# Spectral mixing and a SiLU block: the 32-point transforms of batches 2 to 7 on sums and differences of n and 31-n

## The chip, the cores and the metric

The kernel runs on one core of a Trainium2 chip. The metric is the device time of one execution in microseconds (us). A core has five engines with a queue each: TensorE (matrix products; PE in the profile, with its weight loads as PEld), VectorE (DVE), ScalarE (ACT), GpSimd (POOL) and SyncE (SP, which here only starts transfers). TensorE writes its results to eight banks of PSUM, from where VectorE or ScalarE copies them out. All numbers here are 32-bit floats; each product in the program becomes two matmul records in the profile.

## The reference

```python
# x: (8, 3008, 256), filt_r, filt_i: (1505, 256)
X = np.fft.rfft(x, axis=1)
Y = X * (filt_r + 1j * filt_i)[None]
y = np.fft.irfft(Y, n=3008, axis=1)          # (8, 3008, 256)
# w_in: (256, 2048), w_out: (2048, 256)
h = y.reshape(24064, 256) @ w_in
out = (h * (1 / (1 + np.exp(-h)))) @ w_out
```

Along the sequence of each batch a Fourier transform, a product with a complex filter and the inverse transform; then a two-layer block with SiLU on all 24064 rows.

## The kernel before

**The main stream.** The second part is cut into 48 pairs of token blocks (6 per batch: two halves of the batch, three blocks in each, of 256, 256 and 240 columns), and each pair into 8 steps over the 2048 hidden units: 384 steps, 48 per batch. A step has two generators that take turns in eight rounds (0 to 7): `hidden(step)` (L765) makes 7 products with the first weights into the banks x (`px`) and yz (`pyz`), and `project(step - 1)` (L824) makes 7 products of the step before with the second weights into four accumulators a0 to a3 (`acc`). A 2x2 block product is made from 7 instead of 8 products, so sums and differences run on VectorE in each step: three combines of `pyz` with copied `px` (`g<-pyz,abc`: g0, g2, g1 in that order), one of 512 columns and two more (`finish`, L813). ScalarE makes the copies of `px` and SiLU. With the last step of a pair the accumulators are copied out (`drain`, L849) and GpSimd adds them up (7 additions); SP stores the result. `tokens(pair)` (L755) makes the sums that a new pair needs, on VectorE, at fixed places (L1201).

**The transforms of the next batch** are cut into pieces that are put between these rounds: `put(step, round, piece)`. A piece is emitted into the engines' queues at that place, and each engine works through its queue in order. For batch b, places are relative to step 48 b, so that place -36 lies in the stream of batch b - 1. A sequence of 3008 = 94 x 32 is transformed in two stages each way:

- first forward stage, 94 points: for batches 2 to 7 in three "fold" groups f (`fold`, `stage1_fold`, `evict_fold`; tile `pf`) and two plain groups u = 6, 7 (`stage1`, `evict_t1`; tile `pa`). The products are copied to SBUF (tiles `tf`, `t`), and GpSimd's queue stores them to DRAM as d1[parity, s, re/im, n, channel], n = 0 to 31.
- second forward stage, 32 points over n: `load_t2(g)` (SP's queue) fetches 4 values of s with 64 partitions (re/im and n), and `forward(g)` (L476; tile `pb`) makes 16 products of 64x32 tiles into two banks, for each g of 6. `multiply` and `add` (L495, L514; VectorE) apply the filter.
- first inverse stage, 32 points: `inverse(g, 2)` (L520; tile `pc`) makes 32 products of 32x64 tiles for two g into four banks a0, f, a1, f. `even` (L568) copies two of them on ScalarE, `rows` (L573) makes sums and differences with the other two on VectorE, and GpSimd's queue stores them to DRAM as d2[row, n, h, channel].
- second inverse stage: `load_t4(g)` fetches four n for all rows, `stage3(g)` (L596; tile `pd`) makes 32 products and `evict_y` copies them into `y`, the input of the main stream.

**Order around the change.** PSUM has two free banks ("f"); other pieces borrow banks of the main stream. `open_step(step, pieces)` emits its pieces at the start of a step, after the first two products of `project`, and holds `project` in rounds 0 and 2, so that x and yz (`HIDDEN`) are free for them. Pieces at round 7 of a step that is a multiple of 8 run between two pairs, when accumulators are free; if the step is in `joined`, the next pair's `project` takes a0 and a1 first and a2 later (L833), otherwise a2 first (L836).

```python
        rest = 5 if b == 1 else 6
        open_step(at - 36, *last_part[0](rest), (part["forward"], 0))
        for g, step in ((0, -32), (2, -24), (4, -16)):
            put(at + step, 7, part["inverse"], g, 2)
            if g < 4:
                pending.append((at + step + 7 / ROUNDS, 10 ** 6 + 9, lambda g=g: part["forward"](g + 2, ACCS)))
                joined.add(at + step)
            put(at + step, 7, part["even"], g, 0, 2)
            put(at + step, 7, part["even"], g, 1, 2)
            put(at + step + 1, 5, part["rows"], g, 0, 2)
            put(at + step + 2, 3, part["rows"], g, 1, 2)
```

So step -36 holds `stage3(6)` of the batch before and `forward(0)`; `forward(1)`, `(3)`, `(5)` stand alone in rounds of -35, -27, -20; `forward(2)` and `(4)` follow the inverse in the joined steps -32 and -24 (at -32 with `stage3(7)` between); the inverse at -16 stands alone.

## Time and profile before

| | us |
|---|---|
| three runs | 2574.51, 2575.43, 2577.16 (median 2575.43) |
| span of the profiled execution | 2578.9 |
| first step of the main stream starts | about 81 |
| one batch in the steady part (48 steps) | 312.6, 312.3 |
| L841 `acc`, TensorE busy | 1509.0 |
| L778 `px`, `pyz`, TensorE busy (four groups) | 679.2 + 454.0 + 232.7 + 225.7 |
| L608 `pd`, of which from `t` tiles | 67.3 |
| L509 `multiply`, VectorE busy | 61.6 + 61.3, 90 each of 684 and 681 ns |
| L578 `rows`, VectorE busy | 57.4, 84 of 683 ns |
| L570 `even`, ScalarE busy | 22.5, 42 of 589 ns alone |
| granted TensorE clock, mean | 0.995 |

How to read it: "busy" is the time in which at least one instruction of a group runs; matmuls overlap, so the mean of one (some 380 ns for 256 columns) is not its pace. The timeline has the start and the length of each instruction or run of like instructions, in us from the start of the span, then the engine, the line, what is written and read, and in brackets how long the engine stood idle before and what ended it. A shape such as 64*32 is the part of TensorE's 128x128 array that a matmul takes.

### The profile page before, as it was taken

What the parts mean: (1) busy time and instruction counts of PE and PEld (TensorE: products, weight loads), DVE (VectorE), ACT (ScalarE), POOL (GpSimd) and SP (SyncE); (2) the same over time, 40 slices, a digit from 0 to 9 for tenths busy, and PEclk for the clock granted to TensorE, in tenths of its full rate; (3) what the DMA queues carried; (4) which work ended last, traced back from release to release, by engine and by line L of the source; (5) the groups of instructions that cost most, each with busy time, mean ns of one, the idle gap of its engine ahead of it and who ended that gap; (6) DMA issues with size and microseconds to landing.
All of it is one profiled execution on the core that took longest, in us unless ns stands there. A gap on an engine that the chain in (4) does not pass through costs nothing.

```text
span 2578.9 us, 47033 instructions
## 1 busy us (share of the span) xinstructions
PE 2552.5 (99%) x18810; PEld 2194.7 (85%) x18810; DVE 1594.2 (62%) x3397; ACT 1085.9 (42%) x3009; POOL 427.3 (17%) x670
## 2 busy tenths in 40 slices
PE   8899999999999999999999999999999999999998
PEld 6688888888888888888888888888888888888987
DVE  7866656666666666666656665666665666545544
ACT  2544444444444444444444434444444444444443
POOL 3211111121112111211122111211121112101101
PEclk9899999999999999999999999999999999999999
DMA  9521132222222212222123121321132210200000
GB/s 285 160 65 62 55 84 64 60 75 65 58 63 73 90 38 58 76 77 74 50 58 92 48 74 50 84 76 55 57 82 62 74 42 28 68 14 16 16 9 17
DMA packets 117316, 170.98 MB, mean 66 GB/s; under 512 B 15332, under 2 KB 91076, under 8 KB 116212
## 3 DMA queue, kind: packets, MB, share of 16 engines
q1 hardware_dynamic: 96920, 117.05, 16.3%
q0 software_dynamic: 17328, 45.76, 5.6%
q10 hardware_dynamic: 2848, 5.15, 0.7%
q8 instruction: 148, 2.42, 0.4%
q14 instruction: 72, 0.59, 0.1%
HBM read 96.07 MB, written 81.26 MB: 69 GB/s over the span
## 4 chain that ended last, share of the span: by engine, by line
PE 96%; DMA 3%; ACT 0%; DVE 0%; issue 0%; ACTq 0%; SPq 0%; POOL 0%; POOLq 0%; DVEq 0%
PE acc L841 44%; PE px L778 26%; PE pyz L778 19%; PE pd L608 3%; PE pb L487 2%; PE pc L530 2%; PE pf L454 1%; DMA d<-q 0%; PE pa L374 0%; DMA w_t<-in_x_dram 0%; DMA filt<-in_filt_r_dram 0%; DMA w_t<-d 0%; PE pa L365 0%; DMA d_t<-d_tbl 0%; DMA raw<-in_moe_w_out_dram 0%; DMA t<-d 0%
## 5 line engine op out<-in xcount | busy, mean ns | idle before, releaser
L841 PE MATMUL acc<-g,w_t 128*128 128x256 f32 (+1 forms) x5376 | 1509.0, 375 | 0.4 <-DVE g L749 0.4
L841 PEld LDWEIGHTS acc<-g,w_t 128*128 128x128 f32 x5376 | 1021.6, 190 | 115.8 <-DVE g L749 0.8
L749 DVE TENSOR_TENSOR g<-pyz,abc 128x256 f32<-128x256 f32 (+1 forms) x1152 | 480.0, 417 | 689.3 <-ACT abc L799 395.0
L749 DVE TENSOR_TENSOR g<-g 128x256 f32<-128x256 f32 (+3 forms) x1152 | 599.6, 521 | 196.7 <-ACT g L782 183.6
L778 PE MATMUL px<-ty,w_t 128*128 128x256 f32 (+1 forms) x2304 | 679.2, 376 | 1.1 <-ACT abc L793 0.6
L782 ACT ACTIVATE g<-g 128x256 f32<-128x256 f32 (+1 forms) x1152 | 472.9, 410 | 250.1 <-DVE g L749 250.1
L749 POOL TENSOR_TENSOR s<-s 128x256 f32<-128x256 f32 (+1 forms) x331 | 257.3, 794 | 1768.1 <-DVE s L859 1555.2
L778 PEld LDWEIGHTS px<-ty,w_t 128*128 128x128 f32 x2304 | 433.2, 190 | 64.4 <-issue 6.2
L778 PE MATMUL pyz<-y,w_t 128*128 128x256 f32 (+1 forms) x1536 | 454.0, 377 | 0.0
L778 PEld LDWEIGHTS pyz<-y,w_t 128*128 128x128 f32 x1536 | 283.8, 189 | 47.5 <-DVE g L749 7.0
L793 ACT COPY abc<-px 128x256 f32<-128x256 f32 (+1 forms) x384 | 141.3, 368 | 372.8 <-PE px L778 372.8
L799 ACT COPY abc<-px 128x256 f32<-128x256 f32 (+1 forms) x384 | 141.5, 368 | 338.6 <-PE px L778 337.6
L782 ACT ACTIVATE g<-px 128x256 f32<-128x256 f32 (+1 forms) x384 | 145.8, 380 | 300.7 <-PE px L778 300.7
L778 PE MATMUL px<-y,w_t 128*128 128x256 f32 (+1 forms) x768 | 232.7, 385 | 0.8 <-DVE y L622 0.8
L778 PE MATMUL pyz<-ty,w_t 128*128 128x256 f32 (+1 forms) x768 | 225.7, 376 | 0.2 <-DVE g L749 0.2
L778 PEld LDWEIGHTS px<-y,w_t 128*128 128x128 f32 x768 | 140.4, 190 | 33.0 <-DVE y L628 5.8
L778 PEld LDWEIGHTS pyz<-ty,w_t 128*128 128x128 f32 x768 | 144.6, 190 | 18.8 <-DVE g L749 1.0
L786 ACT COPY abc<-px 128x256 f32<-128x256 f32 (+1 forms) x384 | 135.3, 352 | 52.6 <-PE px L778 52.6
L608 PEld LDWEIGHTS pd<-wi_t,t 48*64 48x64 f32 x3840 | 61.4, 135 | 25.3 <-ACT g L782 16.4
L466 POOL DMA_DIRECT2D d<-tf x144 | 71.4, 503 | 29.7 <-DVE tf L462 29.7
L859 ACT COPY s<-acc 128x512 f32<-128x512 f32 (+1 forms) x94 | 54.2, 577 | 47.6 <-issue 28.6
L582 POOL DMA_DIRECT2D d<-q x84 | 45.7, 547 | 149.6 <-DVE q L578 146.8
(135 smaller groups left out, 1212.9 us busy)
## 6 DMA issues: line engine op xcount, KB each, us to landing
t<-d SPq DMA_DIRECT2D x120, 192.0 KB
t<-d SPq DMA_DIRECT2D x84, 256.0 KB
d<-q POOLq DMA_DIRECT2D x84, 256.0 KB, 2.7
out_dram<-s SPq DMA_DIRECT2D x64, 256.0 KB
d<-tf POOLq DMA_DIRECT2D x144, 96.0 KB, 4.0
xr<-in_x_dram SPq DMA_DIRECT2D x6, 1472.0 KB
out_dram<-s SPq DMA_DIRECT2D x30, 240.0 KB
x_all<-in_x_dram SPq DMA_DIRECT2D x72, 96.0 KB
```

Source lines behind the costliest of these rows:

```text
L466: nc.gpsimd.dma_start(out=d1[k // 2, :, k % 2, n0:n0 + 4], in_=us["tf"][32 * k:32 * k + NS].rearrange("p q n c -> p (q n) c"))
L487: nc.tensor.matmul(out=ps[k][32 * j:32 * j + 32, ri, :], lhsT=d_t[rows, 4 * g + at, ri, :], rhs=rhs, start=True, stop=True)
L530: nc.tensor.matmul(out=ps[j][64 * k:64 * k + 64, a, :], lhsT=e_t[rows, g + a, k, ri, :], rhs=zs[k][rows, ri, :], start=(a == 0 and ri == 0 ...
L608: nc.tensor.matmul(out=ps[h][c0:c0 + 64, cb, i, :], lhsT=t4[rows, i, 128 * cb + c0:128 * cb + c0 + 64], rhs=wi_t[rows, :], start=True, sto ...
L749: eng.tensor_tensor(out=out, in0=in0, in1=in1, op=op)
L778: nc.tensor.matmul(out=out, lhsT=w_t[:, jp, c, 0], rhs=rhs, start=start, stop=True, skip_group_check=True)
L782: nc.scalar.activation(out=g[:, k, 0:n], in_=g[:, k, 0:n] if src is None else src, func=AFT.Silu)
L786: nc.scalar.copy(out=sums[:, 0, 0:n], in_=xo)
L793: nc.scalar.copy(out=sums[:, 1, 0:n], in_=xo)
L799: nc.scalar.copy(out=sums[:, 2, 0:n], in_=xo)
L841: nc.tensor.matmul(out=acc[pair][i][:, h, 0:n], lhsT=w_t[:, jp, c, 1], rhs=g[:, k, 0:n], start=(jp == 0 and h == 0), stop=last, skip_group ...
L859: copy(out=s[:, 2 * i:2 * i + 2, 0:n], in_=acc[pair][i][:, :, 0:n])
```

## The change

Batches 0 and 1 stay as they are. For batches 2 to 7 the values at n and 31 - n are added and subtracted before the 32-point stage, so that each half of them needs 16 cosines or sines in place of 32, for the real and the imaginary part on partitions of their own:

- First stage: the fold groups now hold n = 4f to 4f+3 and their mirror images, and the plain groups u = 6, 7 are mirror images of each other. `evict_fold` copies two of the four banks on ScalarE; `pairs_fold` makes differences and sums with the other two on VectorE (`butterfly`, two operations of 512 columns for each of two halves), and GpSimd's queue stores both (8 stores at once, of the same size as the 8 in two lots before). `pairs_t1` does the same for u = 6, 7 (4 operations on VectorE instead of a copy on VectorE and one on ScalarE for u = 7; 6 stores instead of 4 for the two).
- `forward_two(g)`, for g = 0, 2, 4, takes two groups at once: 32 products of 32x32 tiles into four banks (f, f, x, yz), in opened steps at -36, -28, -20. `free_two` copies the banks x and yz to SBUF on ScalarE. `multiply_two` (8 operations of 512 columns) and `add_two` (4 of 512 instead of 8 of 256) are spread over the step and the three after it.
- `inverse_two(g)` makes 32 products of 32x32 tiles for two groups into four banks, at the places of the old `inverse`, with all three steps joined. `even_two` and `rows_two` are `even` and `rows`; `ends_two` makes the sum and the difference that give n and 31 - n (4 more operations of 512 columns per two groups on VectorE), and the stores follow it.
- `stage3(6)` moves from step -36 to the joined step before (-32), with `stage3(7)`; `stage3` of the second half runs in mirrored order with another table. `load_t4(0)` and `(1)` are issued at -12 instead of -14. Three tables are loaded over the old ones at step 40.

```diff
+        def butterfly(p, q, ps):
+            back = ps[:, ::-1, :]
+            nc.vector.tensor_tensor(out=q, in0=p, in1=back, op=ALU.subtract)
+            nc.vector.tensor_tensor(out=p, in0=p, in1=back, op=ALU.add)
...
+        def forward_two(g):
+            ps = {(k, ri): bank(b, f"pb_{b}_{g}_{k}_{ri}", HIDDEN[ri] if k else None)
+                  for k in range(2) for ri in range(2)}
+            for a in range(2):
+                for j in range(4):
+                    for k in range(2):
+                        par, at = slot_source(k, j)
+                        for ri in range(2):
+                            rows = slice(64 * par + 32 * ri, 64 * par + 32 * ri + 32)
+                            nc.tensor.matmul(out=ps[k, ri][32 * j:32 * j + 32, a, :],
+                                             lhsT=dn_t[rows, 4 * (g + a) + at, :],
+                                             rhs=t2s[g + a][rows, at, :], start=True, stop=True)
+            for a in range(2):
+                t2s.pop(g + a)
+                if g + 2 + a < NG:
+                    load_t2(g + 2 + a)
+            banks[g] = ps
+
+        def free_two(g):
+            out = upool.tile([128, 2, 2, C], FP32, name=f"uc_{b}_{g}", tag="u")
+            for ri in range(2):
+                nc.scalar.copy(out=out[:, ri], in_=banks[g][1, ri])
+                banks[g][1, ri] = out[:, ri]
+
+        def multiply_two(g, k, ri):
+            zs = prods.setdefault(g, {})
+            zs[k, ri] = [pool.tile([128, 2, C], FP32, name=f"{t}_{b}_{g}_{k}_{ri}", tag=t)
+                         for pool, t in ((zpool, "z"), (ppool, "p"))]
+            for m in range(2):
+                nc.vector.tensor_tensor(out=zs[k, ri][m], in0=banks[g][k, ri],
+                                        in1=f_t[m][:, g:g + 2, k, :], op=ALU.mult)
...
+        def inverse_two(g):
+            ps = [bank(b, f"pc_{b}_{g}_{j}", j // 2 if j % 2 == 0 else None) for j in range(4)]
+            zs = prods.pop(g)
+            for ri in range(2):
+                for a in range(2):
+                    for k in range(2):
+                        cols = slice(64 * a + 32 * k, 64 * a + 32 * k + 32)
+                        for j in range(4):
+                            rows = slice(32 * j, 32 * j + 32)
+                            nc.tensor.matmul(out=ps[j][cols, ri, :], lhsT=en_t[rows, g + a, k, ri, :],
+                                             rhs=zs[k, ri][0][rows, a, :], start=True, stop=True)
+            halves[g] = ps, []
...
+        def ends_two(g, i):
+            qt = halves[g][1][i]
+            low = opool.tile([128, 2, C], FP32, name=f"low_{b}_{g}_{i}", tag="o")
+            nc.vector.tensor_tensor(out=low, in0=qt[:, 0], in1=qt[:, 1], op=ALU.add)
+            nc.vector.tensor_tensor(out=qt[:, 0], in0=qt[:, 0], in1=qt[:, 1], op=ALU.subtract)
+            a0 = 8 * g + 8 * i
+            for end, part in ((0, low), (1, qt[:, 0])):
+                nc.gpsimd.dma_start(out=d2[a0:a0 + 8, 16 * end:16 * end + 16], in_=part)
...
-                put(at + step, 7, part["evict_fold"], f, 0)
-                put(at + step, 7, part["evict_fold"], f, 1)
-                put(at + step + 1, 5, part["evict_fold"], f, 2)
-                put(at + step + 1, 5, part["evict_fold"], f, 3)
+                put(at + step, 7, part["evict_fold"], f)
+                put(at + step + 1, 3, part["pairs_fold"], f, 0)
+                put(at + step + 1, 5, part["pairs_fold"], f, 1)
...
-            put(at - 44, 3, part["evict_t1"], 7, 0)
-            put(at - 44, 5, part["evict_t1"], 7, 1)
+            put(at - 44, 3, part["pairs_t1"], 0)
+            put(at - 44, 5, part["pairs_t1"], 1)
...
+    def plan_two(b, part):
+        at = STEPS * b
+        for g, step in ((0, -36), (2, -28), (4, -20)):
+            open_step(at + step, (part["forward_two"], g), (part["free_two"], g))
+            for after, rnd, piece, *args in ((0, 3, "multiply_two", 0, 0), (0, 5, "multiply_two", 0, 1),
+                                             (1, 3, "add_two", 0), (1, 5, "multiply_two", 1, 0),
+                                             (2, 3, "multiply_two", 1, 1), (3, 3, "add_two", 1)):
+                put(at + step + after, rnd, part[piece], g, *args)
+            put(at + step + 4, 7, part["inverse_two"], g)
+            joined.add(at + step + 4)
+            for i in range(2):
+                put(at + step + 4, 7, part["even_two"], g, i)
+            for after, rnd, piece, i in ((5, 5, "rows_two", 0), (6, 3, "rows_two", 1),
+                                         (6, 5, "ends_two", 0), (7, 3, "ends_two", 1)):
+                put(at + step + after, rnd, part[piece], g, i)
+        put(at - 12, 1, part["load_t4"], 0)
+        put(at - 12, 1, part["load_t4"], 1)
...
-            join(at + 16, part, *((7,) if b == B - 1 else (None, 7)))
+            join(at + 16, part, *((7,) if b == B - 1 else (6, 7)))
```

## The prediction, made before the changed kernel ran

> **What bounds the kernel now.** I read the page's busy table and chain of waits first, then the transforms among the groups by shape, then the timeline, step by step, of one batch (b = 5, which repeats every 312.6 us).

> ```profile
> PE 2552.5 (99%) x18810; PEld 2194.7 (85%) x18810; DVE 1594.2 (62%) x3397; ACT 1085.9 (42%) x3009; POOL 427.3 (17%) x670
> PE 96%; DMA 3%; ACT 0%; DVE 0%; issue 0%; ACTq 0%; SPq 0%; POOL 0%; POOLq 0%; DVEq 0%
> L487 PE MATMUL pb<-t,d_t 64*32 64x256 f32 x1344 | 46.0, 382 | 0.0
> L530 PE MATMUL pc<-z,e_t 32*64 32x256 f32 x1344 | 41.6, 380 | 0.0
> ```

> TensorE is the chain, and the two transforms to be cut (pb, pc) hold 88 us of it, 12.5 us a batch. Everything else counts only where TensorE waits for it.

> The unit I count in is the step. A plain step (28 matmul records of 256 columns) takes 6.04 us from its first px<-y matmul to the next step's (5.67 at 240 columns). What an inserted transform costs is the excess over that, in batch 5: step -36 (opened; pd of g=6, then pb) 2.30; pb alone at -35, -27, -20: 1.22 each; -32 (pc, pd, pb) 4.21; -24 (pc, pb) 3.13; -16 (pc alone) 2.11. Sum 15.42 us a batch. pb alone lasts 1.02 from its first weight load to that of the next big matmul, so the switch of tiles adds 0.2; pc alone is 1.91 + 0.2.

> **What the matmuls cost after.** Their records start in bursts of 7 ns, as many as tiles are free, then wait for a wave: pb and pc run 8 at a time, 0.216 us a wave of 256 columns, so 4 waves (32 records) and 8 waves (64). The fold stage already runs 16 tiles (24x32):

> ```profile
> 1399.28 0.66 PE L454 MATMUL pf<-x_all,wq_t 24*32 24x512 f32 x8
> 1399.33 0.66 PE L454 MATMUL pf<-uf,wq_t 24*32 24x512 f32 x8
> 1399.73 0.63 PE L454 MATMUL pf<-x_all,wq_t 24*32 24x512 f32 x8
> 1399.79 0.63 PE L454 MATMUL pf<-uf,wq_t 24*32 24x512 f32 x8
> ```

> Sixteen records start within 0.1 us, sixteen more 0.45 later: two waves of 512 columns. forward_two and inverse_two (64 records of 256 columns, four row groups into four banks, as in pf) are 4 waves each, 1.05 us. Lower bound 0.86 (waves alone); upper 1.91 (8 at a time, as pc); pf is all but the same instruction, so 1.05. That is 3 x 1.05 instead of 6 x 1.02 forward, and 3 x 1.05 instead of 3 x 1.91 inverse.

> **What the change puts behind them.** The old pieces were each other's cover: pb ran while pd or pc was copied out.

> ```profile
> 1420.63 1.15 PE L608 MATMUL pd<-wi_t,t 48*64 48x47 f32 x64
> 1421.71 1.09 PE L487 MATMUL pb<-t,d_t 64*32 64x256 f32 x32
> 1421.87 0.47 ACT L628 COPY y<-pd 128x376 f32<-128x376 f32 x1 [1.09 <-PE pd L608]
> 1422.74 0.70 PE L778 MATMUL px<-y,w_t 128*128 128x256 f32 x2
> ...
> 1557.18 1.98 PE L530 MATMUL pc<-z,e_t 32*64 32x256 f32 x64
> 1559.10 0.70 PE L778 MATMUL px<-y,w_t 128*128 128x256 f32 x2
> 1559.17 1.07 ACT L570 COPY q<-pc 128x512 f32<-128x512 f32 x2 [1.01 <-PE pc L530]
> 1559.63 0.59 PE L841 MATMUL acc<-g,w_t 128*128 128x256 f32 x2
> ```

> In the new opened steps (-36, -28, -20) nothing follows forward_two: the next matmul, px, needs the bank that free_two copies out on ScalarE. From the start T: last matmul into it ends T+1.14, copy T+1.19 (0.05 behind, as pc's) to T+1.78, px at T+1.93 (0.15 behind, as after the pa copy that ends at 1369.58); zo waits for the second copy (two take 1.07) some 0.15 more, part of which the step absorbs. Excess 1.93 + 0.2 + 0.1 = 2.27 us, three times. Queued behind px is all of TensorE. Bounds: 1.25 if the copies were covered, 2.6 if both stood on the path; the row of two copies decides for 2.27.

> At -24 and -16 inverse_two stands alone and the step is "joined", so the first projection goes into bank a0, which even_two copies out: copy T+1.20 to T+1.79, acc at T+1.94 where it could have gone at T+1.40. After what the switch gives back 0.46 is lost: 2.11 - 0.86 + 0.46 = 1.71 each (1.25 if hidden, 2.2 if the second copy counted too). The old -16 put bank a2 first and paid nothing. At -32 pc shrinks by 0.86 and pd of g=6 (1.08) takes pb's place (1.02): 3.41. Its two evictions (0.55 on VectorE, 0.47 on ScalarE) move with it, behind a second pd, before anyone needs a2 and a3.

> Sum: 3 x 2.27 + 3.41 + 2 x 1.71 = 13.64 against 15.42: **1.78 us saved per batch**, not the 5.55 that the waves promise (6 x 1.02 + 3 x 1.91 - 6 x 1.05).

> [...] free_two uses ScalarE alone. [...]

> **VectorE.** Per batch it gains 12 "ends" operations (0.69), 6 more in the folds and 3 in pairs_t1 (0.68), and its additions become 12 x 0.69 instead of 24 x 0.42: about +12 us in 312, hidden where they fit between two of the step's own combines. Per step there are two slots. The rows pair (1.40 listed, 1.32 from start to next start) fits both exactly, even at 240 columns: after the pair at 1462.00 the combine runs at 1463.32, as in a plain step. All new pairs are of this size, one to a slot, but for one place. Order on VectorE shows step -22: after g2's combine the pair of ends_two(2,0), and behind it tokens, in one slot. Before, tokens alone filled it:

> ```profile
> 1518.03 0.42 DVE L749 TENSOR_TENSOR g<-pyz,abc 128x256 f32<-128x256 f32 x1 [0.24 <-ACT abc L799]
> 1518.38 0.68 DVE L749 TENSOR_TENSOR ty<-y 128x512 f32<-128x512 f32 x1
> 1519.09 0.89 DVE L749 TENSOR_TENSOR ty<-y,ty 128x256 f32<-128x256 f32 x2
> 1519.90 0.42 DVE L749 TENSOR_TENSOR g<-pyz,abc 128x256 f32<-128x256 f32 x1
> 1520.37 0.30 PEld L778 LDWEIGHTS pyz<-y,w_t 128*128 128x128 f32 x2 [0.15 <-DVE g L749]
> ```

> There TensorE already waits for the last combine, so a pair more delays it by **1.32 us** a batch; the next step's pyz and everything behind it on TensorE wait. Bounds 0 and 1.40.

> **Moved at no cost.** free_two's 6 ScalarE copies beyond the stall (ScalarE 42% busy). POOL issues the 8 stores of a fold together one round later than its first four before (8 x 0.50 us); for fold 2 the loads of t2(0), t2(1) on SP, which started at 1411.09, start 2 us later: their megabyte lands by about 1419.2, before T = 1420.6. pairs_t1 has 6 stores for 4, with 4 steps to spare. t2(2) to t2(5) are loaded 8 steps ahead (4 issues at once). load_t4(0) and (1), 4 issues, move past two output stores (0.93 us) and behind ends_two's stores: landing about 1585, needed at 1590. Three table loads (0.83 MB, once) at step 40, needed at 60. If these covers fail, the next thing late is pb or pd itself, which stops TensorE.

> **Sum.** 1.78 - 1.32 = 0.46 us a batch, six batches: 2.8 us off the profiled span of 2578.9, which lies 3.5 above the median of the runs; the head before the steps and the tail are not touched. The same difference off the median, 2575.43: **2572.6 us**.

> **Rivals.**
> Faster: the gap at -22 does not open, because the delayed combine is made up by the slack behind it, and the opened steps' copies cost less. Without the 1.32: 2564.7; with the opened steps' 1.02 above 1.25 gone too (3 x 1.02 x 6 = 18) 2546. For it: VectorE idles 38%. Against: in the fence above the wait is already there.
> Slower: the spectrum comes late. If t2's packets share the queue with the output stores behind them (all ended at 1419.41, 2 us later now, plus 0.55 until a waiter starts, as between the stores' end at 1572.56 and 1573.11), forward_two(0) could start only at 1422.0: 1.4 us a batch, 8 in all, 2581. It decides from 1.2 us of lateness on. Against: the loads are first in the queue.
> Not sixteen at a time: 6 x 0.86 a batch, 31 us: 2604. Against: pf.

> **How the numbers follow.** Forecast 48%, faster rival 22%, late spectrum 18%, eight at a time 4%, the rest (small stalls of several slots, mostly slower) 8%. About 0.2% (5.2 us) is what a measurement can tell from no change. The forecast's own range (its stalls, 3 x 1.02 + 2 x 0.46 + 1.32 = 5.3 a batch, a fifth smaller or larger) is 2566 to 2579; a fifth of its chance lies below 2570.3; adding the faster rival: faster 0.31, same 0.39, slower 0.30. Range for 8 in 10: 2559 to 2588; low takes in the -22 gap gone and a third of the opened steps' copies, high the late spectrum with both copies on the path.

> **What would show it.** Records of pb and pc in bursts of sixteen; px waiting for the free_two copy about 0.9 us in each opened step, with excess 2.27; acc waiting for the even copy 0.5 at -24 and -16; pyz waiting 1.3 to 1.5 us for VectorE once a batch, after tokens. Wrong if pb waits for t2, if another slot of VectorE overflows, or if an opened step costs 1.25.

## The result, and the profile after

| | before | changed |
|---|---|---|
| runs beside each other, us | 2574.51 to 2578.17, median 2576.3 | 2588.82 to 2595.43, median 2591.76 |
| ratio, 95% interval | 1 | 1.0063 (1.0049 to 1.0078) |
| span of the profiled execution | 2578.9 | 2587.8 |
| first `px` of step -37 of batch 2 to the first `px` of the last step but one | 2078.6 | 2092.7 |

The changed kernel is 0.6% slower, some 15 us, where 2.8 us less were forecast; 2591.76 lies outside the range of 2559 to 2588. The last row begins where the new pieces begin and leaves out the head, which differs from execution to execution (the main stream starts at 80.4 us before and at 73.9 in the changed kernel's profile): in this row the traces differ by 14.1 us, and this is what has to be explained.

The page of the changed kernel, the busy times and the chain by engine, and from the groups by shape (line, engine, tiles, shape, count | busy us, mean ns | idle before, and what ended it):

```profile
PE 2538.9 (98%) x18810; PEld 2177.6 (84%) x18810; DVE 1668.8 (64%) x3451; ACT 1104.0 (43%) x3039; POOL 442.7 (17%) x682
PE 94%; DMA 3%; DVE 1%; ACT 1%; issue 0%; SPq 0%; POOL 0%; ACTq 0%; POOLq 0%; DVEq 0%
...
L740 PE MATMUL pd<-wn_t,t 48*64 48x47 f32 x3072 | 53.5, 232 | 2.4 <-issue 2.1 <-DVE g L907 0.3
L564 PE MATMUL pb<-t,d_t 32*32 32x256 f32 x1152 | 29.2, 385 | 1.0 <-DMA t<-d 1.0
L602 PE MATMUL pc<-z,e_t 32*32 32x256 f32 x1152 | 26.9, 385 | 0.0
```

TensorE's busy time fell by 13.6 us, and its share of the chain by two points: the shorter transforms are there, and TensorE waits for more than they gave. The idle times over 0.3 us in front of TensorE's instructions, added up over the steps from -36 of batch 2 on, are 23 us, where the kernel before has 0.4 (one wait at the end):

| TensorE waits for | sum, us | where |
|---|---|---|
| ScalarE, first copy of `free_two` | 12.5 | `px` of all 18 opened steps, 0.66 to 0.78 |
| VectorE, a combine | 6.9 | the first `pyz` of step -21, behind the slot at -22, 1.08 in each of six batches (and 0.4 at the end) |
| "issue" | 2.8 | inside `pd`, 4 times: 0.70 and 1.28 at -32 of batches 2 and 4, 0.52 and 0.34 at -8 of batches 3 and 5 |
| a DMA | 0.7 | `pb` at -36 of batch 3 |
| by the view, ScalarE's `evict_y` | 0.5 | `pyz` behind the row at -32 of batch 6 (the last section puts it with the "issue" pauses) |

The timeline of the changed kernel (start, length, engine, line, what is written and read, and in brackets the idle time and what ended it) shows an opened step (-20 of batch 5), a joined one (-24), the slot of VectorE at -22, and -32 of batch 4:

```profile
1530.28 1.49 PE L564 MATMUL pb<-t,d_t 32*32 32x256 f32 x64
1531.79 1.07 ACT L576 COPY uc<-pb 128x512 f32<-128x512 f32 x2 [1.40 <-PE pb L564]
1532.43 0.70 PE L936 MATMUL px<-y,w_t 128*128 128x256 f32 x2 [0.66 <-ACT uc L576]
...
1508.05 1.49 PE L602 MATMUL pc<-z,e_t 32*32 32x256 f32 x64
1509.53 1.07 ACT L608 COPY q<-pc 128x512 f32<-128x512 f32 x2 [0.50 <-PE pc L602]
1510.17 0.70 PE L999 MATMUL acc<-g,w_t 128*128 128x256 f32 x2
...
1522.04 0.69 DVE L907 TENSOR_TENSOR ty<-y 128x512 f32<-128x512 f32 x1
1522.76 0.88 DVE L907 TENSOR_TENSOR ty<-y,ty 128x256 f32<-128x256 f32 x2
1523.57 0.42 DVE L907 TENSOR_TENSOR g<-pyz,abc 128x256 f32<-128x256 f32 x1
1524.04 0.70 PE L936 MATMUL pyz<-y,w_t 128*128 128x256 f32 x2 [1.08 <-DVE g L907]
...
1141.65 1.49 PE L602 MATMUL pc<-z,e_t 32*32 32x256 f32 x64
1143.08 1.96 PE L740 MATMUL pd<-wn_t,t 48*64 48x47 f32 x119
1146.31 0.33 PE L740 MATMUL pd<-wn_t,t 48*64 48x47 f32 x9 [1.28 <-issue]
```

A transform takes 1.49 us from its first record to the modelled end of its last, forward or inverse, where by the same measure one half of the old forward took 1.09 and an old inverse 1.98. Everything behind it waits in the predicted order: copy, then `px` or `acc`. In the fourth group TensorE stops between record 119 and record 120 of `pd` with nothing that this view shows as late.

The late spectrum stands in the same view, at -36 of batch 5 of the kernel before (two lines), of batch 5 of the changed kernel and, last six lines, of its batch 3:

```profile
1407.95 1.97 POOL L466 DMA_DIRECT2D d<-tf  x4 [1.26 <-DVE tf L462]
1411.09 2.79 SPq L473 DMA_DIRECT2D t<-d  x4
...
1412.04 0.52 POOL L527 DMA_DIRECT2D d<-tf  x1 [3.54 <-DVE tf L445]
1415.50 0.50 POOL L527 DMA_DIRECT2D d<-tq  x1
1418.06 2.68 SPq L533 DMA_DIRECT2D t<-d  x4
...
784.21 0.50 POOL L527 DMA_DIRECT2D d<-tf  x1 [2.58 <-issue]
787.85 2.98 SPq L533 DMA_DIRECT2D t<-d  x4
792.01 0.62 PE L564 MATMUL pb<-t,d_t 32*32 32x256 f32 x4
792.87 0.71 PE L564 MATMUL pb<-t,d_t 32*32 32x256 f32 x28 [0.23 <-DMA t<-d]
794.23 0.62 PE L564 MATMUL pb<-t,d_t 32*32 32x256 f32 x4 [0.65 <-DMA t<-d]
795.01 0.71 PE L564 MATMUL pb<-t,d_t 32*32 32x256 f32 x28 [0.15 <-DMA t<-d]
```

In batch 5 SP could start the loads of t2 at 1418.06, 6.4 us ahead of forward_two(0) at 1424.42; before they started at 1411.09, 9.5 us ahead of the opened step's first matmul and 10.6 ahead of `pb`. In batch 3 GpSimd itself paused 2.58 us between its fourth and fifth store, the loads started 4.2 us ahead, and the transform ran in four pieces.

By places, as the prediction counts them (excess over plain steps, us a batch; a step runs from its first `px` to that of the next, so that an opened step's transform, which stands ahead of its `px`, falls into the step before; "undisturbed" is the place where neither t2 nor TensorE's instructions came late):

| place | before | predicted | measured, six batches | undisturbed |
|---|---|---|---|---|
| -36 | 2.30, and 1.22 at -35 | 2.27 | 2.95, 6.40, 2.82, 2.66, 2.83, 2.77 | 2.46 |
| -32 | 4.21 | 3.41 | 4.63, 3.63, 5.12, 3.63, 4.30, 3.94 | 3.63 |
| -28 | 1.22 at -27 | 2.27 | 2.46 in all six | 2.46 |
| -24 and -16 | 3.13, 2.11 | 1.71 each | 1.89 each in all six | 1.89 |
| -20 with the slot at -22 | 1.22 | 2.27 + 1.32 | 3.76 in all six | 3.76 |

### The profile page after: what moved, and what is told of

Its sections match the earlier page's. It is cut to its first block, busy times and chain, and to the rows that moved or that the text cites. A ratio compares the mean times of both kernels' runs of the same rounds, so it can differ in the third digit from the quotient of the medians.

```text
span 2587.8 us, 47087 instructions
## 1 busy us (share of the span) xinstructions
PE 2538.9 (98%) x18810; PEld 2177.6 (84%) x18810; DVE 1668.8 (64%) x3451; ACT 1104.0 (43%) x3039; POOL 442.7 (17%) x682
## 4 chain that ended last, share of the span: by engine, by line
PE 94%; DMA 3%; DVE 1%; ACT 1%; issue 0%; SPq 0%; POOL 0%; ACTq 0%; POOLq 0%; DVEq 0%
PE acc L999 43%; PE px L936 25%; PE pyz L936 19%; PE pd L740 3%; PE pb L564 1%; PE pc L602 1%; PE pf L508 1%; DMA filt<-in_filt_i_dram 0%; PE pa L420 0%; DMA w_t<-in_x_dram 0%; DVE g L907 0%; ACT uc L576 0%; DMA d<-q 0%; DMA w_t<-d 0%; DMA t<-d 0%
## 5 line engine op out<-in xcount | busy, mean ns | idle before, releaser
L936 PE MATMUL px<-y,w_t 128*128 128x256 f32 (+1 forms) x768 | 234.0, 386 | 13.2 <-ACT uc L576 12.5
L740 PEld LDWEIGHTS pd<-wn_t,t 48*64 48x64 f32 x3072 | 49.1, 135 | 21.2 <-ACT g L940 15.9
L623 POOL DMA_DIRECT2D d<-low x36 | 22.1, 615 | 214.2 <-DVE low L619 214.2
L740 PE MATMUL pd<-wn_t,t 48*64 48x47 f32 x3072 | 53.5, 232 | 2.4 <-issue 2.1
```

What stands on the lines that cost most here:

```text
L740: nc.tensor.matmul(out=ps[h][c0:c0 + 64, cb, 3 - i if back else i, :], lhsT=t4[rows, i, 128 * cb + c0:128 * cb + c0 + 64], rhs=table[rows, ...
L936: nc.tensor.matmul(out=out, lhsT=w_t[:, jp, c, 0], rhs=rhs, start=start, stop=True, skip_group_check=True)
```

## The experiments

All are edits of the changed kernel but the last, each timed beside the kernel before in five executions or more; "saved" is the difference of its ratio from 1.0063, times 2576 us. The intervals are some 0.13% to either side, and that of 1.0063 itself (1.0049 to 1.0078) is common to all: of the single edits only tokens_later, no_copy and stage3_apart lie clear of it, stores_two_queues touches it, and for the rest the places in the trace decide. The savings by the medians are 0.9 to 4.5 us above those of the traces (over the last row of the first table), in part because the changed kernel's profiled execution, 2589.6, lies 2.2 below its median.

**tokens_later**: the sums for the new pair one slot later.

```diff
-    combines = ((-2, 1), (6, 1), (11, 5), (22, 5), (26, 6), (38, 1))
+    combines = ((-2, 1), (6, 1), (11, 5), (22, 5), (27, 5), (38, 1))
```

> The change with one edit: the tokens of pair 4 of each batch are made at (27, round 5) instead of (26, round 6), so that the pair of ends_two(2, 0) has its slot on VectorE for itself. Theory of place: the wait of pyz for VectorE (1.08 us of TensorE idle, 1.3 in the step) vanishes once a batch, 7.9 us in six batches: 2584 where the change took 2592. Rival, VectorE simply has too much to do: the wait comes back one step later, and the time moves by less than 2.

Measured: 2585.31 us, ratio 1.0032 (1.0020 to 1.0045), 8.0 us saved. From -22 to -19 the trace is 8.1 us shorter, 6 x 1.35, and the wait of `pyz` is gone. The overflow of one VectorE slot cost what the prediction said.

**stores_two_queues**: four of the eight stores of fold 2 go to SP's queue.

```diff
-                    nc.gpsimd.dma_start(out=d1[par, :, grp, at:at + 4],
+                    queue = nc.sync if f == 2 and part is us["q"] else nc.gpsimd
+                    queue.dma_start(out=d1[par, :, grp, at:at + 4],
```

> The change with one edit: of the eight stores of the last fold (f = 2) the four of the differences go through SP's queue instead of GpSimd's. Theory of the late spectrum: the loads of t2(0), t2(1) start 2 us earlier, forward_two(0) at -36 no longer waits within itself, and its excess (2.66 to 6.40 us over the six batches in the changed kernel's trace) falls to 2.45: 5 to 6 us less, 2586. Rival, the transfers themselves are slow and not their issue: 0 to 2 us less.

Measured: 2584.45 us, ratio 1.0036 (1.0022 to 1.0049), 7.0 us saved. Its timeline at -36 of batch 3:

```profile
777.84 1.53 SPq L528 DMA_DIRECT2D d<-tq  x4
778.82 1.99 POOL L528 DMA_DIRECT2D d<-tf  x4 [3.55 <-DVE tf L445]
782.45 2.73 SPq L534 DMA_DIRECT2D t<-d  x4
...
791.20 1.49 PE L565 MATMUL pb<-t,d_t 32*32 32x256 f32 x64
793.36 0.70 PE L937 MATMUL px<-y,w_t 128*128 128x256 f32 x2 [0.66 <-ACT uc L577]
```

The loads start 8.7 us ahead of the transform, it runs in one piece, and the step up to the `px` at -36 takes 9.15 us in all six batches (9.18 to 11.48 before this edit); with the step behind it in batch 3 that is 5.6 us less. So the queue of stores, not the loads themselves, made the spectrum late, and in five of the six batches (in batch 7 by 0.02), not only where a wait is over 0.3 us.

**no_copy**: `free_two` is left out, and the filter of the second half reads the banks of the first; the copies out of x and yz, and with them half of the spectrum, are not in this time.

```diff
-            open_step(at + step, (part["forward_two"], g), (part["free_two"], g))
+            open_step(at + step, (part["forward_two"], g))
...
-                nc.vector.tensor_tensor(out=zs[k, ri][m], in0=banks[g][k, ri],
+                nc.vector.tensor_tensor(out=zs[k, ri][m], in0=banks[g][0, ri],
```

> The change without free_two: its copies are left out, and the filter products of the second half read the banks of the first half (that part of the result is left out). Theory of the lost cover: px starts 1.42 us after forward_two's first matmul instead of 2.15, and pyz has no copy to wait for: 0.85 us in each of 18 opened steps, 15 us less: 2576. Rival, the sixteen-tile matmuls themselves (their slow issue and the switch of tiles) hold TensorE: less than 4 us.

Measured: 2579.12 us, ratio 1.0013 (1.0004 to 1.0022), 12.9 us saved. The timeline of -28 of batch 5:

```profile
1471.15 1.49 PE L564 MATMUL pb<-t,d_t 32*32 32x256 f32 x64
1472.69 0.67 PE L936 MATMUL px<-y,w_t 128*128 128x240 f32 x2
```

An opened step costs 1.76 now instead of 2.46 (at -28): the copies were worth 0.70 us of it. But 1.76 is far from the 1.25 that the prediction gave a covered transform: `px` starts 1.54 us after the first record, not 1.05. By the traces 12.0 us are saved, of the 15 expected. Without any copy, and with the other losses left in, the change would still not have won.

**acc2_first**: only the joined step -32 keeps the order a0, a1, a2.

```diff
-            joined.add(at + step + 4)
+            if g == 0:
+                joined.add(at + step + 4)
```

> The change with -24 and -16 taken out of the joined steps, so that the next pair starts with bank a2 as the old -16 did. Theory: the wait of acc for the even copy (0.40 us of weight-load idle) vanishes at both places, 0.3 us each, 12 of them: 3.5 us less, 2588. Rival, the wait only moves to the next product into a0 two products later: under 1 us.

Measured: 2589.97 us, ratio 1.0050 (1.0037 to 1.0063), 3.3 us saved. Behind the inverses at -24 and -16 a step is 6.15 us long instead of 6.41, 12 x 0.26 = 3.2 us in all; the rest of the trace differs by how late the spectrum came (1.6 us longer) and by the pauses in `pd` (0.4 longer), so that the whole is 1.2 us shorter. The wait of 0.40 for the even copy cost 0.26, not 0.46.

**x_first**: in the transform's second half (a = 1) the records of bank x come first, then yz.

```diff
-                for j in range(4):
-                    for k in range(2):
-                        par, at = slot_source(k, j)
-                        for ri in range(2):
+                for k in (1, 0):
+                    for ri in range(2):
+                        for j in range(4):
+                            par, at = slot_source(k, j)
```

> forward_two orders the records of its second half (a = 1) so that those of bank x come first, then yz, then the two f banks; nothing else changes. Theory: in an opened step px waits for the copy of bank x, which starts 0.02 us after the last of the 64 records has ended (T + 1.49), because the second 32 records start only every 15 ns and those of x are spread over all of them. With x first, its last record starts near T + 0.77 and ends near T + 1.14; copy to T + 1.75; px at T + 1.80 instead of T + 2.15: 0.35 us in each of 18 opened steps, 6 us, some 2585.5 where the changed kernel has 2591.8 (ratio 1.0037 to before). Rival: the order within the second half decides which tiles are free, and with it the sixteen no longer run together (up to 0.4 us an opened step lost): 2592 to 2599.

Measured: 2587.34 us, ratio 1.0043 (1.0031 to 1.0056), 5.2 us saved. The timeline of -20 of batch 5:

```profile
1529.32 1.49 PE L564 MATMUL pb<-t,d_t 32*32 32x256 f32 x64
1530.65 1.07 ACT L576 COPY uc<-pb 128x512 f32<-128x512 f32 x2 [1.21 <-PE pb L564]
1531.29 0.70 PE L936 MATMUL px<-y,w_t 128*128 128x256 f32 x2 [0.48 <-ACT uc L576]
```

The copy starts 1.33 after the first record instead of 1.51 and `px` waits 0.18 less, in each of 18 steps, half of the 0.35 expected; the whole trace is 3.1 us shorter. The expectation had taken a product's two records as neighbours, so that the four products of bank x would have been the first 8 records of the half. In the trace the record that signals bank x is the 20th of the half and starts at 0.92 us: all 16 first records of a half (0.46 to 0.87) start ahead of all second ones (0.88 to 1.12).

**stage3_apart**: `stage3(6)` leaves -32 and stands alone one step ahead of forward_two(0).

```diff
-            if b == B - 1:
-                alone_at(at + 11, 3, part, 6)
-            join(at + 16, part, *((7,) if b == B - 1 else (6, 7)))
+            alone_at(at + 11, 3, part, 6)
+            join(at + 16, part, 7)
```

> stage3(6) leaves the joined step -32 and stands alone in round 3 of step -37, in the two f banks, as the last batch has it already. Theory: the pauses of TensorE in pd at -32 that wait for nothing the profile shows (0.34 to 1.28 us, 2.8 us in the profiled execution) come from 192 small records in a row (pc 64, pd 64, pd 64), which use up the instructions that lie ready; with 64 and 128 in a row they vanish: some 2589 (ratio 1.005). Rival: they belong to the place or to a number of instructions since the last jump, and stay or move to the next small records: 2592, with issue pauses of 2 to 4 us again; and a transform on its own costs 0.2 us more at the switch, 1 us in all.

Measured: 2584.23 us, ratio 1.0031 (1.0020 to 1.0043), 8.2 us saved, more than expected; by the trace 5.8, and mostly for another reason. At -32 the delays are gone, 2.8 us in batches 2, 4 and 7 and 0.7 behind the row in batch 6; the piece alone costs 1.22 a batch where in the row it cost 0.93, which takes back 1.8. The larger part, 4.1 us, is gained at -36: the piece stands ahead of forward_two(0) again, as it did in the kernel before, so that the loads of t2 start 7.7 us ahead of the transform in batch 5 instead of 6.4. The expectation had put all four "issue" pauses at -32; two of them are at -8, where the row is 32 records of `pf` and 128 of `pd`, and there they stay (0.20 in batch 3, 0.81 in batch 5). The kernel before has a trace of them at the same place: its steps at -8 cost 3.46 and 3.76 in batches 3 and 5 where they cost 3.38 in batches 2, 4 and 6.

**one_after**: of the two products of `project` ahead of forward_two one is emitted after it.

```diff
-            for _ in range(2):
+            for _ in range(1 if step in late else 2):
                 next(work[1])
         until(step - 0.05)
+        if step in late:
+            next(work[1])
```

> In the opened steps of forward_two the second product of project that was emitted before the transform is emitted after it, ahead of px. Theory: it fills 0.43 of the 0.66 us in which TensorE waits for the first copy of free_two; 18 x 0.43 = 7.7 us at most, some 2585 (ratio 1.0035). Rival: that product was itself the cover under which banks x and yz came free for the transform (the copy of px on ScalarE and the last combine on VectorE), so that the wait only moves ahead of pb: 2592, with pb waiting 0.3 to 0.5 us in each opened step.

Measured: 2588.99 us, ratio 1.0046 (1.0033 to 1.0058), 4.4 us saved. `px` no longer waits over 0.25 us in any opened step, and the steps at -28 and -20 are shorter by 0.29 and 0.33. At -36 both theories hold: the transform starts earlier and waits 2.2 us for t2 in the trace instead of 0.7 (waits over 0.3 us), so that these steps are 0.5 us longer in sum. The whole trace is 3.4 us shorter.

**copy_two_engines**: `free_two`'s second copy on VectorE.

```diff
-                nc.scalar.copy(out=out[:, ri], in_=banks[g][1, ri])
+                copy = nc.vector.tensor_copy if ri else nc.scalar.copy
+                copy(out=out[:, ri], in_=banks[g][1, ri])
```

> free_two's second copy (bank yz) goes to VectorE, the first (bank x) stays on ScalarE. Theory: only the first copy stands on the path of px, and the second is covered by px itself, so nothing is gained: 2591 to 2593, with px waiting 0.66 us as before; VectorE has 0.7 us more in each opened step, which may cost up to 0.3 us there (2597). [...]

Measured: 2587.9 us, ratio 1.0042 (1.0029 to 1.0056). The median is 5.4 us lower, but its interval overlaps that of the changed kernel, and the trace shows only 0.06 to 0.08 us an opened step and is 0.9 us shorter in all; `px` waits 0.66 as before. The median does not settle the theory; by the trace the first copy alone is waited for.

**mends_b** (tokens_later, stores_two_queues, acc2_first, x_first, stage3_apart), **mends_c** (the same with one_after) and **mends_d** (with copy_two_engines too); the edits are those shown.

> The changed kernel with tokens_later, stores_two_queues, acc2_first, x_first and stage3_apart together. Theory: the losses are separate waits in separate places and their removals add up, but for the late spectrum, which stores_two_queues and stage3_apart both remove. From the traces, over the six batches: 8.1 (tokens) + 5.6 (late spectrum) + 3.2 (a2 first) + 3.2 (x first, 18 x 0.18) + 1.1 (pd apart: 8.4 saved at -32, 7.3 paid at -37) = 21 us, so some 2570.5 (ratio 0.998). Rival: as TensorE is never idle for the same reason twice in a step, the gaps closed open again behind (VectorE or ScalarE late elsewhere) and half comes back: 2580.

> mends_b, and one project product after forward_two as in one_after. Theory: of the 0.48 us that px still waits for the copy of bank x, a product of 0.43 fills what the start of the transform, 0.43 earlier, doesn't take back: 0.2 us in 18 opened steps, 3.6 us: some 2567 (ratio 0.9964). Rival: the earlier start makes pb wait for the banks x and yz or for t2 (it did for t2 in one_after, 2.2 us in all): no gain, 2570 to 2572.

> mends_c, and free_two's second copy on VectorE as in copy_two_engines. Theory: by the trace of copy_two_engines px still waits for the first copy alone, so nothing changes: within 2 us of mends_c. [...]

| | median, us | ratio (95%) | last row of the first table, us |
|---|---|---|---|
| mends_b | 2567.63 | 0.9971 (0.9960 to 0.9982) | 2070.4 |
| mends_c | 2560.16 | 0.9937 (0.9925 to 0.9950) | 2062.9 |
| mends_d | 2556.68 | 0.9929 (0.9916 to 0.9941) | 2061.8 |

The savings add up: 22.3 us in the trace of mends_b for 21 expected. mends_c gains 7.5 more, twice what was expected, 0.41 a step: with t2 in time and x first, the whole product (0.43) lies where TensorE waited. Whether mends_d is better still, its 1.1 us in the trace and the overlapping intervals leave open. Its opened step at -20 of batch 5, in the timeline:

```profile
1512.81 1.68 PE L565 MATMUL pb<-t,d_t 32*32 32x256 f32 x64
1514.14 0.58 ACT L578 COPY uc<-pb 128x512 f32<-128x512 f32 x1 [0.69 <-PE pb L565]
1514.39 0.69 DVE L578 COPY uc<-pb 128x512 f32<-128x512 f32 x1 [0.21 <-PE pb L565]
1514.41 0.70 PE L1002 MATMUL acc<-g,w_t 128*128 128x256 f32 x2
1514.95 0.59 PE L939 MATMUL px<-y,w_t 128*128 128x256 f32 x2
```

The copy of x lies beside `acc`, and `px` follows without a wait. mends_c and mends_d are faster than both kernels: the change pays, 0.6 to 0.7%, once what it brought along is taken away.

**before_tokens**: the edit of tokens_later in the kernel before.

> The kernel before with tokens at step 27, round 5, in place of step 26, round 6: the one of the mends that has something to act on there (its stores, its order of banks and its transforms are the old ones, and its TensorE waits for none of them). Theory: the mends take back what the change brought with it; the kernel before loses only 0.16 to 0.25 us a batch at this slot, so 1 to 1.5 us in all: 2574 to 2576 (ratio 0.9995). Rival: the place of tokens is bad in itself, and the kernel before gains as much as the changed one did, 8 us: 2567.

Measured: 2575.3 us, ratio 1.0003 (0.9994 to 1.0012): nothing. That place cost nothing until the change put a pair of operations ahead of it. The other mends were not tried in the kernel before; its TensorE has 0.4 us of waits over 0.3 us that they could take away.

## Why the prediction was wrong, by its steps

The miss in the traces is 14.1 + 2.8 = 17 us. By the table of places: lateness at -36 5.7, pauses at -32 3.5 and at -8 1.0, the transforms with their copies 6.7 (12 x 0.18 at the joined steps, 18 x 0.18 at the opened ones, 6 x 0.22 at -32). Each of these three alone turns the forecast gain of 2.8 into a loss, and without any one of them the time would have come out inside the range (2591.8 less the 4.5 of the pauses is 2587.3).

- **"Moved at no cost" failed: 0 taken, 5.7 us measured.** The prediction let the loads of t2(0) and t2(1) start 2 us later and land at 1419.2, ahead of T = 1420.6, where the transform starts once `stage3(6)` has left the step. Against T they started 3.2 us later in batch 5 and 5.4 in batch 3 (GpSimd paused between stores there). The transfer itself took what the prediction had given it: counted in the traces, the 1024 packets of 1 KB that t2(0) and t2(1) make up had ended 6.0 us after the first load started in batch 5, and 6.1 in the kernel before. stores_two_queues takes the lateness away by an earlier start (5.6 us), stage3_apart most of it by a later transform (4.1). 1.7 of the 5.7 lie in the step behind the broken transform of batch 3, where the granted clock fell (last section). What the prediction named as a sign of being wrong, `pb` waiting for t2, is there. The late spectrum, given 18% and 8 us, was real, for the reason of the stores and not of the shared load queue that the rival named.
- **The size of a sixteen-tile transform was wrong: 1.05 taken from its first record to the next matmul, 1.54 measured without the copies (no_copy).** "`pf` is all but the same instruction" held for 32 records, and a transform has 64. Their starts in the trace, from the first record: 16 within 0.10 us, 16 from 0.24 to 0.34, one at 0.46, and the remaining 31 from 0.65 to 1.12, one each 16 ns. The first half comes in bursts of sixteen as predicted; the second comes at a pace. So the last record ended at T + 1.49 and the copy started at T + 1.51, where the prediction had T + 1.14 and T + 1.19. Between 1.05 and the 1.91 of eight at a time nothing was priced.
- **That an opened step came out at 2.46, near the 2.27 predicted, is in part luck**: the transform alone cost 1.76 where 1.25 stood, and the copies 0.70 where 1.02 stood, so that two errors took each other back. The terms of the 2.27 as printed, 1.93 + 0.2 + 0.1, make 2.23.
- **The copies cost 0.70 of an opened step, not 1.02** (no_copy). The mechanism, first copy ahead of `px`, second not on the path, was right; with the late start of the copy a part of what the prediction put down to the copy was the transform. Copying out of PSUM is what TensorE waits for in all 18 opened steps, 12.5 us in the changed kernel's trace. That both copies stand on the path, as the high end of the range has it, no run shows: putting them on two engines gave 0.9 us in the trace (copy_two_engines), while a product laid over the copy (one_after) and an earlier start of it (x_first) gave 3 to 5 each.
- **-24 and -16: right mechanism, 1.89 for 1.71.** The wait of `acc` costs 0.26, not 0.46; the transform without it 1.63, not 1.25 (acc2_first).
- **-32: 3.41 predicted, 3.63 undisturbed, 4.2 as measured.** The pauses at this row, which no term covered, made the difference; the row of 192 small records came from moving `stage3(6)`, and without it in the row they are gone there (stage3_apart). What the traces show of them is told in the last section.
- **The slot at -22 was right to the number**: 1.32 predicted, 1.35 saved by tokens_later. The rival that had it vanish (22% with the cheaper copies) fell. Eight at a time fell, by the bursts.

The range failed because it took the unknown stalls one at a time: its high end held the late spectrum together with both copies on the path, not the late spectrum together with the longer transform and the pauses.

## What to carry to other kernels

When a piece is moved away from in front of another, price what it had covered: the transfer behind it, not only the piece's own time. Check a burst rate on as many records as the new piece has, not on the half of them that a neighbour shows. And price what the copy out of PSUM behind a small transform leaves uncovered: with the other losses mended but `px` still waiting for the copy the change gained 0.3% (mends_b), with one product laid over the copy 0.6% (mends_c).

## What was not expected of the hardware

- After 32 records of 32x32 tiles, with their 32 weight loads, the next started one each 16 ns, in both orders that were run (changed kernel and one_after; x_first); in the kernel before, with 64x32 or 32x64 tiles, 8 started in each 0.216 us, 27 ns each, so that such a pace could not have shown. What sets it no run varied.
- After the broken transform of batch 3 the granted clock fell to half. The windows of the changed kernel (window: length, busy time of PE, PEld, DVE, ACT and POOL, then the granted clock, DMA share and GB/s):

```profile
792.00:797.00 5.00, 3.19 (x67) 1.06 (x67) 0.69 (x1) 1.24 (x3) 0.00 (x0) 1.00 1.04 275
797.00:799.00 2.00, 2.00 (x6) 1.65 (x6) 0.69 (x2) 0.37 (x1) 0.00 (x0) 0.50 1.07 225
799.00:801.00 2.00, 2.00 (x8) 1.66 (x7) 1.69 (x4) 0.69 (x2) 0.00 (x0) 0.65 0.45 97
```

  TensorE is busy all through the second and third, with 6 and 8 matmuls where 801 to 803, at full clock, has 11 by the same view; the step behind the transform, from `px` to `px`, takes 7.00 us instead of 5.34. No single idle time there is over 0.8 us; five microseconds in which TensorE was busy for 3.2 went ahead of it; whether they made the clock fall no run shows.
- TensorE's "issue" pauses differ from batch to batch and from kernel to kernel at one and the same place, and the traces tell where they stand. The changed kernel's view of its transfers has a queue that carries instructions alone, in 147 packets of 16 KB each:

```profile
q8 instruction: 147, 2.41, 0.4%
```
